# Strassen's algorithm in the first channel product of two more chunks, with turns between VectorE and GpSimd

## The chip, the core and the metric

The kernel runs on one core of one Trainium2 chip. Five engines run beside each other, each with its own queue of instructions that it works off in order: TensorE (PE; its weight loads are shown as PEld), VectorE (DVE), ScalarE (ACT), GpSimd (POOL) and SyncE (SP). They wait for each other by semaphores. Only TensorE multiplies matrices, and it writes to PSUM; VectorE and ScalarE read PSUM, GpSimd works in SBUF alone. The metric is the device time of one execution in microseconds.

## What is computed

The reference is a linear attention with random features (8 batches, 8 heads, 576 positions, head size 64, 128 features), followed by a mixer over tokens and over channels:

```python
def phi(x):
    proj = np.einsum('bhsd,md->bhsm', x, omega)
    sq = np.sum(x * x, axis=-1, keepdims=True) / 2.0
    h = proj - sq
    h = h - np.max(h, axis=-1, keepdims=True)
    return np.exp(h) / np.sqrt(m)
q_p, k_p = (phi(q_s), phi(k_s))
kv = np.einsum('bhsm,bhsd->bhmd', k_p, v)
z = np.sum(k_p, axis=2)
num = np.einsum('bhsm,bhmd->bhsd', q_p, kv)
den = np.einsum('bhsm,bhm->bhs', q_p, z)[..., None] + 1e-06
x = num / den                                # heads side by side: 576 x 512 for each batch
h = np.maximum(x.T @ w_tok1, 0.0) @ w_tok2   # tokens, 576 -> 256 -> 576
u = x + h.T
out = u + np.maximum(u @ w_ch1, 0.0) @ w_ch2 # channels, 512 -> 1536 -> 512
```

## The kernel before

Matrices are held in fp16, sums in fp32. For each batch b there are three stages. **Attention** (`attention`): for each of four pairs of heads, TensorE projects k and q (`kp`, `qp`, lines 679 and 691) and the last 64 positions (`kt`, `qt`, 571 and 641); ScalarE takes the exponentials; VectorE takes the largest entry (`km`), GpSimd scales v by its reciprocal (`vs_`, by the helper in line 315); TensorE forms `kv` (735, 742) and the numerators (768, 770), and VectorE or ScalarE divides. **Token mixing** (`token_mix`): lines 796 and 803, a relu, line 816, and `uadd` on VectorE; a SyncE transpose (`ut_dma`) turns `u` into `uT`; `token_tail` (870) does the last 64 positions of two batches. **Channel mixing** (`channel_mix`): 512 positions of a batch make a chunk, and the 64 left over from each of eight batches make a ninth, so there are nine, c = 0 to 8.

The first channel product of a plain chunk is 12 blocks of four matmuls of 512 columns (line 1144), each with one relu from PSUM (helper lines 310 and 312). From c = `FAST_IN` on it goes by `channel_in_fast`: the product is cut in two by two by two, four sums of `uT` blocks are made (`go`, engine chosen, helper line 315), then seven products of four matmuls of 256 columns in each of three parts (line 1073 records those matmuls and line 1097 the joins). ScalarE copies three products out of PSUM (`keep`), VectorE adds them to others (`join`), and relus work from PSUM or within SBUF. It needs eight sums of blocks of `w_ch1` (`weight_sums`), made once; they take the place of one of three q slots and one of three k slots. From c = 1 on the second product goes by a Strassen form too, with eight sums `S` of relu outputs for each chunk (`channel_out_fast`, line 961; reads in line 941); four sums of `w_ch2` blocks (line 468) are made once. Chunk 0 uses lines 1150, 1152 and 1178.

From batch 2 on, q and k come in by two DMAs: GpSimd issues a cast from fp32 to a DRAM scratch (for k one for the main part and two small ones for the tail), and SyncE issues a transpose back to SBUF (`qT`, `kT`, line 400). GpSimd also issues the loads of v and its tails (lines 357 and 371).

The order of all work is written out by hand. `Planner.add` makes numbered jobs, each with an engine, dependencies and buffers; `ORDER` lists their numbers, `SLOT` the buffer that each takes, `MOVED` the jobs whose engine is not the usual one. `Planner.run` emits them in the order of `ORDER`, so each engine's queue is its part of that list. Negative numbers are dummy matmuls that fill the start.

Of the kernel before, what the change touches and what calls it, by code (L numbers as in the profile page):

```python
# [92 lines left out]
]  # L93
# [44 lines left out]
class Planner:  # L138
# [8 lines left out]
    def add(self, eng, cost, key, fn, deps=(), take=(), give=(), rows=False, wire=0.0):  # L147
        job = Job(eng, cost, key, fn, [d for d in deps if d is not None], list(take), list(give), rows, wire)
        self.jobs.append(job)
        return job  # L150

    warm = None

    def run(self):
        slots = iter(SLOT)
# [30 lines left out]
def kernel(  # L186
# [12 lines left out]
    nc = tc.nc  # L199
# [135 lines left out]
    ld = {}  # L335
# [915 lines left out]
```

## Time and profile before

| what | value |
|---|---|
| three runs | 274.83, 275.26, 275.27 us; median 275.26 |
| the profiled execution | 273.79 us, of which the span of the trace is 272.0 |
| granted TensorE clock | 0.998 |
| VectorE / ScalarE / GpSimd busy | 227.2 / 164.2 / 134.6 us |
| DMA | 39.70 MB, mean 146 GB/s |

A line of the profile names a line of the kernel, an engine, an operation and the tiles it writes and reads; "x28" is a count. Matmuls are pipelined, so the mean time of one is longer than the spacing from one to the next; the chain of waits, which gives the time of a run of matmuls, shows the spacing. Helper lines (306, 310, 312, 315, 534) stand for many uses, which are told apart by tile and shape.

### The profile page before, as it was taken

How to read it: one execution, taken by the hardware profiler on the slowest of the kernel's cores; microseconds unless marked ns; L12 is line 12 of the kernel's file. 1: busy time of each engine (PE TensorE's matmuls, PEld its weight loads, DVE VectorE, ACT ScalarE, POOL GpSimd, SP SyncE). 2: the span in 40 equal slices, each digit the busy share in tenths (PEclk: the TensorE clock that was granted, in tenths of full speed). 3: DMA queues.
4: the chain of work that ended last, by engine and by line, in shares of the span. 5: the costliest groups of instructions: out<-in, count | busy, mean ns of one | idle time of the engine just before them, and what ended most of it. 6: DMA issues, size and time to landing. Idle time of an engine off the chain costs nothing.

```text
span 272.0 us, 6648 instructions
## 1 busy us (share of the span) xinstructions
PE 262.9 (97%) x2647; PEld 180.0 (66%) x2647; DVE 227.2 (84%) x479; ACT 164.2 (60%) x361; POOL 134.6 (49%) x146
## 2 busy tenths in 40 slices
PE   7799999999999999999999999999999999999992
PEld 4367455444568655766578546986789688888881
DVE  3897879876998799987889799899997795799992
ACT  2999941188695338736746865699947541573500
POOL 8895492064803490079459996964145044600001
PEclk9999999999999999999999999999999999999999
DMA  8999999999999999989989986980260063030134
GB/s 199 190 208 210 191 210 185 216 202 132 180 204 156 223 187 175 164 160 158 171 178 173 194 233 64 182 167 2 49 128 2 23 193 58 0 157 0 63 133 119
DMA packets 81296, 39.70 MB, mean 146 GB/s; under 512 B 63984, under 2 KB 77040, under 8 KB 81072
## 3 DMA queue, kind: packets, MB, share of 16 engines
q0 software_dynamic: 31744, 17.74, 44.2%
q1 hardware_dynamic: 46928, 15.37, 29.5%
q10 hardware_dynamic: 2592, 6.16, 6.4%
q8 instruction: 20, 0.33, 0.5%
q14 instruction: 12, 0.10, 0.1%
HBM read 35.95 MB, written 16.52 MB: 193 GB/s over the span
## 4 chain that ended last, share of the span: by engine, by line
PE 86%; DMA 8%; POOL 3%; DVE 1%; issue 0%; POOLq 0%; SPq 0%
PE bank L961 24%; PE bank L1144 19%; PE bank L1073 13%; PE bank L803 5%; PE bank L816 5%; DMA uT<-u 4%; DMA w1m<-in_moe_w_tok_dram 4%; PE bank L1178 4%; PE bank L679 3%; PE bank L768 3%; PE bank L735 3%; PE bank L691 2%; POOL r L339 1%; PE bank L870 1%; PE bank L842 1%; PE bank L854 1%
## 5 line engine op out<-in xcount | busy, mean ns | idle before, releaser
L1144 PE MATMUL bank<-uT,wc 128*128 128x512 f16 x232 | 56.0, 379 | 0.0
L315 POOL TENSOR_TENSOR vs<-v,vs 128x512 f16<-128x512 f16 x31 | 33.1, 1072 | 42.8 <-DVE vs L716 33.5
L310 ACT ACTIVATE r<-bank 128x512 f16<-128x512 f32 (+1 forms) x61 | 34.5, 598 | 26.5 <-PE bank L1144 16.0
L961 PEld LDWEIGHTS <-r 128*128 128x128 f16 x384 | 36.7, 98 | 7.2 <-issue 1.6
L534 ACT ACTIVATE kp<-bank 128x512 f16<-128x512 f32 x64 | 35.5, 623 | 9.6 <-PE bank L679 8.9
L712 DVE TENSOR_REDUCE km<-kp 128x8 f16<-128x1024 f16 x32 | 38.5, 1204 | 2.0 <-ACT kp L534 2.0
L534 ACT ACTIVATE qp<-bank 128x512 f16<-128x512 f32 x64 | 36.5, 620 | 4.3 <-PE bank L691 4.3
L1144 PEld LDWEIGHTS <-wc 128*128 128x128 f16 x232 | 20.5, 98 | 20.1 <-issue 1.1
L961 PEld LDWEIGHTS <-S 128*128 128x128 f16 x288 | 27.7, 98 | 4.7 <-issue 0.4
L786 DVE TENSOR_TENSOR x<-bank,rc 128x320 f16<-128x320 f32 x53 | 25.2, 483 | 1.1
L941 DVE TENSOR_TENSOR o<-u,bank 128x512 f32<-128x512 f16 x28 | 19.1, 680 | 5.8 <-PE bank L961 5.3
L961 PE MATMUL bank<-T,r 128*128 128x256 f16 x192 | 23.8, 273 | 0.0
L961 PE MATMUL bank<-T,S 128*128 128x256 f16 x192 | 23.4, 272 | 0.0
L961 PE MATMUL bank<-wc,r 128*128 128x256 f16 x192 | 23.1, 273 | 0.0
L312 DVE TENSOR_SCALAR r<-bank 128x512 f16<-128x512 f32 (+1 forms) x29 | 18.9, 661 | 3.1 <-PE bank L1144 2.4
L819 DVE TENSOR_TENSOR u<-x,bank 128x512 f16<-128x512 f16 x28 | 17.9, 681 | 1.9 <-PE bank L816 1.9
L315 POOL TENSOR_TENSOR vbd<-vt,vbd 128x512 f16<-128x512 f16 x6 | 6.4, 1060 | 23.5 <-DVE vbd L616 18.5
L768 PEld LDWEIGHTS <-qp 128*128 128x128 f16 x256 | 14.0, 98 | 5.9 <-issue 0.3
L1073 PE MATMUL bank<-uT,wc 128*128 128x256 f16 x120 | 16.6, 273 | 0.6 <-DMA uT<-u 0.6
L941 DVE TENSOR_TENSOR o<-o,bank 128x512 f32<-128x512 f32 x21 | 14.3, 680 | 3.1 <-PE bank L961 2.9
L775 DVE RECIPROCAL rc<-bank 128x5 f32<-128x5 f32 x64 | 11.2, 184 | 6.7 <-PE bank L770 3.7
L768 PE MATMUL bank<-kvsb,qp 128*128 128x65 f16 x256 | 16.0, 193 | 0.2 <-ACT qp L534 0.2
(151 smaller groups left out, 551.3 us busy)
## 6 DMA issues: line engine op xcount, KB each, us to landing
out_dram<-o ACTq DMA_DIRECT2D x9, 512.0 KB, 3.7
q<-in_q_dram POOLq DMA_DIRECT2D x6, 576.0 KB, 7.6
wc<-in_moe_w_ch_dram POOLq DMA_DIRECT2D x4, 768.0 KB, 11.1
k<-in_k_dram POOLq DMA_DIRECT2D x6, 512.0 KB, 7.1
v<-in_v_dram POOLq DMA_DIRECT2D x6, 512.0 KB, 8.6
out_dram<-o SPq DMA_DIRECT2D x5, 512.0 KB, 3.1
r<-in_q_dram POOLq DMA_DIRECT2D x4, 288.0 KB, 7.1
v<-in_v_dram POOLq DMA_DIRECT2D x4, 256.0 KB, 8.9
```

What stands on the lines that cost most here:

```text
L310: nc.scalar.activation(out=out, in_=in_, func=AF.Relu)
L312: nc.vector.tensor_relu(out=out, in_=in_)
L315: (nc.gpsimd if eng == "POOL" else nc.vector).tensor_tensor(**kw)
L534: nc.scalar.activation(out=out, in_=in_, func=AF.Exp, bias=0.0, scale=1.0)
L712: nc.vector.reduce_max(out=t_km[place("km", (b, hp))], in_=src_, axis=AX.X)
L768: nc.tensor.matmul(ps[:, k, j * 65 : (j + 1) * 65], st, s[:, i, 0 : D + 1], start=True, stop=True)
L786: nc.vector.tensor_tensor(out=to, in0=ps, in1=rc.unsqueeze(2).broadcast_to((P, NJ + 1, D)), op=ALU.mult)
L819: nc.vector.tensor_tensor(out=t_u[place("u", b)][:, j, :], in0=t_x[place("x", b)][:, j, :], in1=bank(n), op=ALU.add)
L941: nc.vector.tensor_tensor(out=o, in0=a, in1=ps, op=ALU.add)
L961: nc.tensor.matmul(ps[:, j * DH : (j + 1) * DH], a[:, cb, j * P : (j + 1) * P], w[:, cb, :], start=(bank_of(b, j0) not in held and j == j0 ...
L1073: nc.tensor.matmul(ps[:, n, :], w(a)[:, (2 * m + n) * P : (2 * m + n + 1) * P], x_[:, a], start=(what in ("P1", "P2", "P5") and n == 0 and ...
L1144: nc.tensor.matmul(ps, wc1[:, db, cb * P : (cb + 1) * P], moving(db), start=(db == 0), stop=(db == ND - 1))
```

## The change

1. `FAST_IN` goes from 5 to 3: chunks 3 and 4 take `channel_in_fast` as well. With c = 5 to 8 that makes six of nine.
2. Jobs that read and write SBUF alone carry `port=True`: the sums `S`, the input sums, the weight sums, the relus within SBUF, and from batch 2 on the mask product, `vbd` and `vs_`. When such a job on one of VectorE and GpSimd is emitted, its first instruction is made to wait for the last such instruction that the other engine was given before it in the order, unless that was waited for already. This gives 53 waits: 26 of VectorE for GpSimd, 27 of GpSimd for VectorE.
3. `ORDER`, `SLOT` and `MOVED` are new from the end of batch 1's attention on. Before that only the banks of three groups of dummy matmuls change.

What differs by count of jobs (engine by engine):

| job | VectorE | ScalarE | GpSimd | TensorE |
|---|---|---|---|---|
| output sums `S` | 54 to 36 | | 10 to 28 | |
| input sums of `uT` | 3 to 11 | | 13 to 13 | |
| weight sums | 0 to 3 | | 8 to 5 | |
| products of the fast first stage | | | | 84 to 126 |
| `keep` | | 36 to 54 | | |
| `join` | 36 to 54 | | | |
| relus of the fast first stage | 12 to 22 | 24 to 32 | | |
| plain blocks of line 1144 | | | | 58 to 34 |
| their relus | 21 to 14 | 39 to 22 | | |
| `kv` copies, divisions, token relus | 69 to 63 | 41 to 47 | | |

The weight sums now begin right after the sums of `w_ch2` blocks, during batch 1's token mixing. Three places of the new queues:

- GpSimd, after the load of v of batch 2: a weight sum, which by its turn waits for VectorE's first weight sum; two tail casts of k of batch 3; a weight sum; the main cast of k of batch 3. TensorE's first use of that `kT` is `kt` of batch 3, among chunk 1's blocks.
- GpSimd, in chunk 1's output sums: one sum, the load of v of batch 3, two sums that need the relu of chunk 1's last block, the tail casts of k of batch 4. Its first use, `kp` of batch 4, stands behind chunk 1's product number seven.
- GpSimd, in chunk 2's output sums: tail casts of k of batch 6, the load of v of batch 5, a sum which waits its turn for chunk 3's last input sum, then a tail of v, the main cast of k of batch 7, a tail of v, tail casts of batch 7, a tail of v, the main cast of k of batch 6. First use: `kp` of batch 6, behind batch 4's token mixing.

```diff
-    def add(self, eng, cost, key, fn, deps=(), take=(), give=(), rows=False, wire=0.0):
+    def add(self, eng, cost, key, fn, deps=(), take=(), give=(), rows=False, wire=0.0, port=False):
         job = Job(eng, cost, key, fn, [d for d in deps if d is not None], list(take), list(give), rows, wire)
+        job.port = port
         self.jobs.append(job)
         return job
...
+    def turns(self, tc, nc):
+
+        engines = {"DVE": mybir.EngineType.DVE, "POOL": mybir.EngineType.Pool}
+        last = {}
+        after = mybir.DependencyInfo(mybir.DependencyClass.Sync, mybir.DependencyReason.DATA)
+        def go(job):
+            traced = nc.cur_bb.bb.instructions
+            n = len(traced)
+            job.fn()
+            if not job.port or job.eng not in engines:
+                return
+            new = [i for i in nc.cur_bb.bb.instructions[n:] if i.engine == engines[job.eng]]
+            other = last.get("POOL" if job.eng == "DVE" else "DVE")
+            if other is not None:
+                tc.add_manual_dep(new[0], other, after, reason="shared port")
+                last["POOL" if job.eng == "DVE" else "DVE"] = None
+            last[job.eng] = new[-1].name
+        self.go = go
...
-            j.fn()
+            self.go(j)
...
-    FAST_IN = 5
+    FAST_IN = 3
...
-                job = add(e_sum, 0.5, key + KEYS["S"] + 0.1 * g + 0.01 * k, go, deps=[*need, *([done[2 if k == 3 else 0]] if k else [])], take=[("S", c)])
+                job = add(e_sum, 0.5, key + KEYS["S"] + 0.1 * g + 0.01 * k, go, deps=[*need, *([done[2 if k == 3 else 0]] if k else [])], take=[("S", c)], port=True)
...
+    plan.turns(tc, nc)
     plan.run()
```

More of the change, by code (lines that the diff above doesn't have):

```diff
@@ L34 @@
     282, 283, 358, 179, 264, 198, 181, 34, 233, 267, 199, 234, 235, 231, 232, 284, 188, 265, 266, 193, 268, 269,
[58 rows of a table removed]
[61 rows of a table added]
 ]
 SLOT = (
-    "0100234050600701103402521706330511460210051223125233033711610240602131270511342163750420056150672712"
-    "4605012137512011365072310230040171020353162243332500316157113242670140235273510446726122030716211530"
-    "7621001035170301612430750012215233641100337415107203005261712324105603750146637054100201605373160221"
-    "3417034617220102300111410160112206212373120413000601312612072013361501345061372705416110302172426125"
-    "0604507130102321004112560270223610715300247200023170141501702032545031703240514062231700400322171045"
-    "1630001075212431053730213210145021011523301212643571030160001741260005120136543035461200711622730510"
-    "0462010341720112126245172201331264025010007101214723236350421705243520532047661402771131116005027134"
-    "6012520463170425116120203004715211601405130720326031400562210513204760123120501236071104220156031131"
-    "71007022247131421062510023034007621125"
+    "0100234050600701103402521706330411560210041223124233033711610250603121207411353126040437052140673012"
+    "5204713106413711024063317200050161037340122250333407012146110052260152204363517456732122006012034206"
+    "0112004512014603230510141121151420235233010325061020417312116252100326541710123150434662015207174621"
+    "0123005436001230112322251340111623050116220154211006022524117603021526747406153206714010530032175621"
+    "4322230107232615370315120060750131021160412201131761151321322204625602725301126051000062151007236143"
+    "2100150174322123135026700124611002507036040310151126074102215110400123304712462013170267302053200101"
+    "3271130205760131002220531060410072232110154361071206302340157164107113202500172761036245560343703011"
+    "3506211470332472121670020403751100621050127310062000167234107612031622707605471011070014570134152001"
+    "6710232732011762530700460315211304201035170402"
 )
@@ L107 @@
     122: "ACT", 128: "ACT", 139: "ACT", 147: "DVE", 149: "DVE", 153: "DVE", 157: "ACT", 159: "DVE", 167: "DVE",
-    171: "DVE", 173: "DVE", 175: "ACT", 179: "DVE", 185: "DVE", 191: "ACT", 197: "ACT", 206: "ACT", 207: "ACT",
-    208: "DVE", 229: "ACT", 246: "ACT", 289: "DVE", 314: "DVE", 322: "DVE", 350: "ACT", 396: "DVE", 413: "DVE",
-    439: "DVE", 466: "DVE", 468: "DVE", 472: "DVE", 474: "DVE", 527: "DVE", 544: "DVE", 606: "DVE", 610: "DVE",
-    616: "DVE", 620: "DVE", 628: "POOL", 629: "POOL", 630: "POOL", 632: "POOL", 647: "ACT", 648: "ACT",
@@ L112 @@
-    677: "DVE", 694: "DVE", 697: "ACT", 728: "DVE", 731: "ACT", 739: "DVE", 750: "DVE", 758: "DVE", 764: "DVE",
-    770: "DVE", 772: "DVE", 776: "POOL", 780: "POOL", 795: "ACT", 828: "ACT", 848: "ACT", 876: "DVE", 879: "ACT",
-    899: "POOL", 900: "POOL", 901: "POOL", 902: "POOL", 903: "POOL", 904: "POOL", 905: "POOL", 906: "POOL",
-    907: "POOL", 908: "POOL", 909: "POOL", 910: "POOL", 925: "ACT", 926: "ACT", 942: "ACT", 958: "ACT",
-    962: "POOL", 981: "ACT", 1011: "DVE", 1017: "ACT", 1028: "DVE", 1051: "ACT", 1062: "DVE", 1083: "POOL",
@@ L117 @@
-    1084: "POOL", 1085: "POOL", 1086: "POOL", 1100: "DVE", 1101: "ACT", 1117: "ACT", 1118: "ACT", 1133: "ACT",
-    1134: "ACT", 1135: "POOL", 1139: "POOL", 1142: "POOL", 1157: "ACT", 1158: "ACT", 1190: "ACT", 1238: "DVE",
-    1244: "ACT", 1261: "POOL", 1262: "POOL", 1263: "POOL", 1264: "POOL", 1278: "DVE", 1294: "DVE", 1311: "ACT",
-    1312: "ACT", 1335: "ACT", 1336: "ACT", 1342: "POOL", 1359: "ACT", 1360: "ACT", 1376: "ACT", 1391: "ACT",
+    171: "DVE", 173: "DVE", 175: "ACT", 179: "DVE", 185: "DVE", 196: "ACT", 197: "ACT", 201: "ACT", 207: "ACT",
@@ new lines @@
+    208: "DVE", 229: "ACT", 246: "ACT", 308: "DVE", 320: "DVE", 326: "DVE", 327: "POOL", 328: "POOL", 329: "POOL",
+    330: "POOL", 331: "POOL", 334: "POOL", 350: "ACT", 379: "DVE", 396: "DVE", 441: "DVE", 458: "DVE", 462: "DVE",
+    468: "DVE", 470: "DVE", 474: "DVE", 478: "POOL", 479: "POOL", 480: "POOL", 481: "POOL", 527: "DVE",
+    533: "ACT", 544: "DVE", 564: "ACT", 567: "ACT", 581: "ACT", 589: "DVE", 602: "POOL", 603: "POOL", 604: "POOL",
+    605: "POOL", 607: "POOL", 627: "ACT", 643: "ACT", 660: "ACT", 662: "POOL", 664: "POOL", 668: "POOL",
@@ new lines @@
+    683: "ACT", 684: "ACT", 736: "ACT", 747: "DVE", 767: "ACT", 785: "POOL", 786: "POOL", 787: "POOL", 818: "DVE",
+    820: "ACT", 837: "POOL", 838: "POOL", 840: "POOL", 843: "POOL", 844: "POOL", 859: "ACT", 909: "ACT",
+    923: "DVE", 929: "ACT", 964: "POOL", 965: "POOL", 966: "POOL", 981: "ACT", 982: "ACT", 998: "ACT",
+    1014: "ACT", 1016: "POOL", 1018: "POOL", 1022: "POOL", 1037: "ACT", 1107: "ACT", 1118: "DVE", 1139: "POOL",
+    1140: "POOL", 1141: "POOL", 1157: "ACT", 1174: "ACT", 1194: "POOL", 1196: "POOL", 1198: "POOL", 1213: "ACT",
@@ L121 @@
+    1214: "ACT", 1260: "DVE", 1263: "ACT", 1277: "DVE", 1297: "ACT", 1336: "ACT", 1350: "DVE", 1351: "ACT",
+    1352: "ACT", 1368: "ACT", 1372: "POOL", 1376: "POOL", 1391: "ACT", 1392: "ACT", 1397: "POOL", 1398: "POOL",
+    1399: "POOL", 1400: "POOL", 1414: "DVE", 1415: "ACT", 1432: "ACT", 1447: "ACT", 1452: "POOL", 1456: "POOL",
 }
@@ L621, in kt_mask @@
                 )
-            j_ktm = add("DVE", 0.15, kkt + 0.01, kt_mask, deps=[j_ktm, j_msk], take=take_vbd, give=[("kmt", b)])
+            j_ktm = add("DVE", 0.15, kkt + 0.01, kt_mask, deps=[j_ktm, j_msk], take=take_vbd, give=[("kmt", b)], port=b >= 2)
             def vbd():
@@ L631, in attention @@
             e_vbd = engine("POOL")
-            j_vbd = add(e_vbd, 1.05 if dma_in else 1.95, kkt + 0.02, vbd, deps=[j_ktm, *ld["vt", b]], give=[("vt", b)])
+            j_vbd = add(e_vbd, 1.05 if dma_in else 1.95, kkt + 0.02, vbd, deps=[j_ktm, *ld["vt", b]], give=[("vt", b)], port=b >= 2)
         j_tail = [j_vbd0, *j_kte] if b == 0 else [j_vbd]
@@ L703, in attention @@
             if b in HALVES:
-                j_h = [add("DVE", 0.35, at_["km"], km_half, deps=je, take=[("vs", (b, hp))])]
+                j_h = [add("DVE", 0.35, at_["km"], km_half, deps=je, take=[("vs", (b, hp))], port=True)]
             else:
@@ L727, in vs_ @@
                 )
-            j_v = add(e_vs, 1.07, at_["vs"] - (6.0 if b == 0 else 0.0), vs_, deps=[j_m, ld["v", b, hh[0]], ld["v", b, hh[1]]], give=[("v", b)])
+            j_v = add(e_vs, 1.07, at_["vs"] - (6.0 if b == 0 else 0.0), vs_, deps=[j_m, ld["v", b, hh[0]], ld["v", b, hh[1]]], give=[("v", b)], port=b >= 2)
             def kv(hp=hp, n_kv=n_kv):
@@ L951, in base_in @@
                 tt(e_base, out=o, in0=t_u[place("u", c)][:, 2 * i : 2 * i + 2, DH * e : DH * e + DH], in1=o, op=ALU.add)
-            return add(e_base, 1.1, key + KEYS["c2"] + step * k, base_in, deps=deps, give=[("u", c)])
+            return add(e_base, 1.1, key + KEYS["c2"] + step * k, base_in, deps=deps, give=[("u", c)], port=True)
         outs, j_z = {}, {}
@@ L1028, in weight_sums @@
                 n = 2 * i + a
-                done.append(add(e_sum, 0.46, key, go, deps=[*need, *j_wc1], take=[("qT" if n < 3 else "kT", "sums")] if n < 6 else []))
+                done.append(add(e_sum, 0.46, key, go, deps=[*need, *j_wc1], take=[("qT" if n < 3 else "kT", "sums")] if n < 6 else [], port=True))
             j_sums.append(done)
@@ L1043, in go @@
                 tt(e_sum, out=sums()[:, i], in0=a(), in1=b(), op=ALU.subtract)
-            j_s.append(add(e_sum, 0.35, key, go, deps=[*jt, *([j_s[i // 2]] if i % 2 else [])], take=[("uT", ("sums", c))]))
+            j_s.append(add(e_sum, 0.35, key, go, deps=[*jt, *([j_s[i // 2]] if i % 2 else [])], take=[("uT", ("sums", c))], port=True))
         half_c = DC // 2
@@ L1119, in relu1 @@
                 relu_to(e_relu, t, t)
-            c1 = add(e_relu, 0.35, kk, relu1, deps=[c11, c12], take=[("r3", c)])
+            c1 = add(e_relu, 0.35, kk, relu1, deps=[c11, c12], take=[("r3", c)], port=True)
             e_relu = engine("DVE")
@@ L1123, in relu22 @@
                 relu_to(e_relu, r3(1, 1, m), r3(1, 1, m))
-            c2 = add(e_relu, 0.2, kk, relu22, deps=[c22], take=[("r3", c)])
+            c2 = add(e_relu, 0.2, kk, relu22, deps=[c22], take=[("r3", c)], port=True)
             for n in range(2):
```

125 rows, old and new, of the table ORDER are left out of this document.

## The prediction

> **What bounds the kernel now.** I read the page first, then each engine's busy time over the long middle, TensorE's waits there, and the chain of waits for the price of one step.
>
> ```profile
> PE 262.9 (97%) x2647; PEld 180.0 (66%) x2647; DVE 227.2 (84%) x479; ACT 164.2 (60%) x361; POOL 134.6 (49%) x146
> PE 86%; DMA 8%; POOL 3%; DVE 1%; issue 0%; POOLq 0%; SPq 0%
> 55.00:267.00 212.00, 211.35 (x2076) 150.75 (x2071) 183.54 (x383) 129.87 (x281) 100.87 (x98) 1.00 0.72 132
> 74.30:211.70 137.40, 137.06 (x1400) 94.16 (x1396) 120.94 (x258) 92.42 (x213) 77.11 (x74) 1.00 0.85 148
> PE bank L1073 <- DMA uT<-u: 0.6, 2, 0.3
> PEld L1073 <- DMA uT<-u: 0.5, 1, 0.5
> ```
>
> From 55 to 267 us TensorE is busy 211.35 of 212.00 us at a granted clock of 1.00, and the only wait of its own worth naming is about 1 us for two transposed `uT` tiles. So matmul time taken out there comes off the end in full, as long as nothing new arrives late; by the same rows there is no slack to hide a late operand in. VectorE is next: 120.94 of 137.40 us between 74.3 and 211.7, that is 88%.
>
> The unit prices, from the chain of waits (start, time, instruction, count):
>
> ```profile
> 47.34 0.32 PE bank L796 x2
> 47.67 1.83 PE bank L803 x8
> 49.50 1.73 PE bank L1178 x8
> 51.23 1.73 PE bank L816 x8
> 55.12 0.45 PE bank L679 x16
> 59.37 0.55 PE bank L870 x4
> 59.92 0.32 PE bank L691 x2
> 66.80 0.24 PE bank L735 x8
> 67.05 0.06 PE bank L742
> 68.27 0.12 PE bank L768 x4
> 68.39 0.03 PE bank L770
> 74.10 0.22 PE bank L641 x2
> 81.82 0.22 PE bank L571 x4
> 117.51 4.32 PE bank L1144 x20
> 234.62 10.04 PE bank L1073 x92
> 253.84 13.11 PE bank L961 x120
> ```
>
> **TensorE.** A plain chunk has 48 matmuls of 512 columns at 4.32/20 = 0.216 us; by Strassen it has 7 x 12 = 84 of 256 columns at 10.04/92 = 0.1091. For chunks 3 and 4: 96 x 0.216 = 20.74 us go, 168 x 0.1091 = 18.33 come, **-2.4 us**, all on the path. The changed warm-up matmuls only swap banks: nothing.
>
> **The other engines.** Rows by shape (busy, mean ns | idle before):
>
> ```profile
> L1097 DVE TENSOR_TENSOR r<-r,bank 128x512 f16<-128x512 f32 x12 | 8.1, 680 | 1.0 <-PE bank L1073 0.9
> L315 DVE TENSOR_TENSOR S<-S,r 128x768 f16<-128x768 f16 x16 | 8.8, 553 | 0.1
> L315 DVE TENSOR_TENSOR uT<-uTt 128x512 f16<-128x512 f16 x2 | 0.8, 418 | 0.0
> L312 DVE TENSOR_SCALAR r<-bank 128x512 f16<-128x512 f32 x27 | 18.1, 679 | 2.7 <-PE bank L1144 2.4 <-PE bank L803 0.2
> L312 DVE TENSOR_SCALAR r<-r 128x1024 f16<-128x1024 f16 x5 | 2.0, 420 | 0.0
> L315 POOL TENSOR_TENSOR S<-r 128x768 f16<-128x768 f16 x3 | 4.9, 1637 | 13.5 <-PE bank L961 11.1 <-ACT r L310 2.4
> L310 ACT ACTIVATE r<-bank 128x512 f16<-128x512 f32 x59 | 33.8, 605 | 26.5 <-PE bank L1144 16.0 <-PE bank L803 10.1 <-issue 0.2
> ```
>
> VectorE gains 18 joins (12.2 us), 8 input sums (3.3), 10 relus within SBUF (at most 0.42 each, 4.2) and 3 weight sums (1.7), 21.4 us; it loses 18 output sums (9.9), 7 chunk relus (4.8) and some 6 small PSUM reads, which I price at 0.42 each, 2.5: 17.2 us. So **+4 us** on VectorE. GpSimd gets 18 output sums and gives up 3 weight sums: 15 x 1.637 = **+25 us**, of 137 us that it is idle now. ScalarE gets 18 copies and 8 relus for 17, some 9 at 0.605 and a few more: +5 to +9, of 108 idle. By totals all of it fits; 88% on VectorE becomes some 91% in the middle. For the lost overlaps I take +0.6 us.
>
> **The turns.** Counted in the new order, 53 waits: 26 of a VectorE sum for a GpSimd sum, 27 the other way. Behind a waiting VectorE sum stand the joins and PSUM reads, for which TensorE waits; behind a waiting GpSimd sum stand the casting loads of q, k and v, for which SyncE's transposes and then TensorE wait. What a collision costs without turns is shown once (VectorE, then GpSimd):
>
> ```profile
> 158.34 1.08 DVE L616 TENSOR_TENSOR vbd<-kmt,mask 128x8 f16<-128x8 f16 x1
> 157.74 1.64 POOL L315 TENSOR_TENSOR sum<-wc,qT 128x768 f16<-128x768 f16 x1
> ```
>
> The tiny mask product ends at 159.42, 0.04 us after GpSimd's sum, so a sum that comes second is held until the other has ended, and a semaphore makes it wait for the same end. So a turn adds only where the written order differs from the order of readiness: between -0.9 us (a collision of this kind avoided) and +1.64 (a whole GpSimd sum) each; I take nothing beyond the 0.6 above. The Trainium skill, SBUF — State Buffer, section "Who interferes with whom", has the same lock, and its Perfetto Trace Analysis, section "Optimizing Scalar/DVE Operations", warns that moving work between these two may not help; by that warning the 18 moved sums gain VectorE nothing, and it would stand at +14 us and not at +4. The row agrees on the lock; the warning is weighed as a rival below.
>
> **The loads in the new order** decide. Now TensorE waits for no k tile; in the new order three of them stand hard against their first use. Landing times, issue costs, and VectorE's last sum of W2 blocks:
>
> ```profile
> k<-in_k_dram POOLq DMA_DIRECT2D x6, 512.0 KB, 7.1
> k<-in_k_dram POOLq DMA_DIRECT2D x12, 32.0 KB, 6.8
> kT<-k SPq DMA_TRANSPOSE x6, 6.5
> DMA to landing us min/median/max: 5.0/6.5/9.0
> L371 POOL DMA_DIRECT2D vt<-in_v_dram x16 | 10.7, 674 | 0.3 <-POOL vbd L315 0.3
> L390 POOL DMA_DIRECT2D k<-in_k_dram x12 | 10.2, 856 | 0.0
> L384 POOL DMA_DIRECT2D k<-in_k_dram x6 | 3.5, 576 | 0.0
> 48.34 0.95 DVE L468 TENSOR_TENSOR T<-wc,T 128x1536 f16<-128x1536 f16 x1
> ```
>
> *Batch 3.* The first weight sum (0.55) follows that sum: 49.84. GpSimd waits for it (a turn), does a weight sum, two tail casts, a weight sum (2 x 1.64 + 2 x 0.86): 54.84. Cast of k: 61.9; transpose: 68.4. TensorE, from 47.34: one L796 0.32, two L803 groups 1.83, four of L816 1.73, seven thirds of L1178 6.05, four kp 1.8, three qp 0.96, kt and qt 0.44, token tail 0.55, eight blocks of chunk 1 6.92, two kv 0.6: 21.2, so 68.5. On time by 0.1; with the transpose's ends 1.6 early to 2.4 late.
>
> *Batch 4.* Its tail cast stands on GpSimd behind two output sums of chunk 1 that need that chunk's last relu. From the end of that block: relu 0.61, two sums 3.27, first tail issued 0.86, landing of the second 6.8, transpose 6.5: 18.0; a load of v and another sum before them can add some 0.7. TensorE has until its first use six numerators 0.9, kp 1.8, four qp 1.28, six output products 7.87, L796 0.32, L803 1.83, qt 0.22, L816 1.73, four kv 1.2: 17.15. **Late by 0.9 to 1.6**; with the transpose's ends -0.6 to +4.1.
>
> *Batch 6.* Its cast stands behind an output sum of chunk 2 that waits its turn for chunk 3's last input sum; between are four issues of 0.67 to 0.86, another cast and a third v tail. From that input sum: 0.42 + 1.64 + 3 x 0.67 + 2 x 0.86 + 0.58 + 7.1 + 6.5 = 20.0, and 0.9 for the load ahead of the sum if GpSimd is behind; TensorE has 13 products 5.67, six output products 7.87 and attention and token parts 7.2: 20.8. On time by the median, but the cast now follows another of 512 KB at once: between 1.3 early and 3 late.
>
> Early pays nothing and late is paid in full, so places near zero cost on average half their scatter: I take 0.3, 1.5 and 1.0, **+2.8 us**. The two late `uT` of now stay.
>
> **Sum.** -2.4 + 0.6 + 2.8 = **+1.0 us**. The profiled execution took 273.79 us (272.0 span and 1.8 around it), 0.5% under the median of 275.26 of the three runs; its sum would give 274.8, and on the median **276.3 us**.
>
> **Rivals.** *Faster.* The three tiles land at the short ends of their rows and stay hidden; the same cast-and-transpose chains end in time all through the present trace, where TensorE waits for no kT. Then -2.4 is left, or -1.0 with one place 1.4 late: 272.9 to 274.5. It decides below 1.8 us of lateness in all. For it speaks that VectorE's and GpSimd's totals fit; against, that batch 4 is late by its medians. *VectorE bound.* The 26 turns hold VectorE 0.5 us each on average, half of the collision's 0.9 or somewhat more: 13 us, and the 4 added, against 28.5 us that it is idle from 55 to 267, most of which is waiting for TensorE. Some 2 us of it then reach TensorE on top of the loads: 278 to 279. The page's warning is this case. *A wash.* The loads give back just the 2.4: 274.7 to 275.8.
>
> **How the numbers follow.** About 0.2% (0.55 us) can be told from no change. Forecast (late kT tiles, +0.6 to +3) 0.38; VectorE bound 0.12; both slower: 0.50. Faster 0.40, a wash 0.10. Likeliest case's own range 275.9 to 278.3; holding 8 in 10 takes most of the faster case and the start of the VectorE case: 273.0 to 278.6.
>
> **What would show it.** Right: TensorE's idle time before L679 or L571, released by `kT<-k`, some 2 to 4 us in all; the Strassen products of the first stage at 504 matmuls (336 now) of 0.109 us; VectorE's busy time up by about 4, GpSimd's by 25. Wrong: no such wait and a span of 269.6 (loads early), or waits of L961 and L1073 for VectorE or GpSimd sums of several us (turns).

## The result, and the profile after

The kernel after took 277.29 us (median of 17 runs, 275.08 to 283.88), the kernel before beside it 274.83. The ratio is 1.0086 with a 95% interval of 1.0059 to 1.0112: slower by some 2.4 us. The forecast was 276.3, and 1.0 us more than before. Two more comparisons of the same kernel gave 276.54 us (ratio 1.0059, 1.0033 to 1.0085) and 277.89 (1.0114, 1.0069 to 1.0159); the ratios leave out executions more than 1.5% above the fastest of their kernel, which the medians include.

The profiled execution took 278.06 us with a span of 276.3. The change moves the line numbers used here by 24: 679 is now 703, 961 is 985, 1073 is 1097, 315 is 339. From its page, busy time by engine and the chain of waits:

```profile
PE 263.5 (95%) x2719; PEld 187.5 (68%) x2719; DVE 228.5 (83%) x487; ACT 173.5 (63%) x384; POOL 158.0 (57%) x161
PE 67%; DMA 14%; POOL 7%; DVE 7%; SPq 2%; issue 2%; POOLq 0%; DVEq 0%
```

There are 72 matmuls more, 168 for 96, as the change says. The chain of waits, 86% TensorE before, is 67% TensorE now, and what came in is DMA, GpSimd and VectorE. TensorE's own waits (us in all, times, longest) name the operands:

```profile
PE bank L531 <- DMA r<-in_q_dram: 1.9, 2, 1.6
PE bank L703 <- DMA kT<-k: 1.7, 2, 1.2
PE bank L1168 <- DMA uT<-u: 1.4, 1, 1.4
PE bank L1097 <- DVE r L1121: 0.4, 1, 0.4
PE bank L595 <- DVE u L843: 0.4, 1, 0.4
```

The first line is a load of q some 10 us after the start, ahead of the new order. It is 0.2 us in the kernel before, and the two later profiles of the kernel after don't have it. The two waits for `kT` are batch 4's (1.2) and batch 2's; the `uT` is batch 1's, which the first product of channel chunk 1 reads. None of these last four lines is in the kernel before, whose two short waits for a `uT` (0.6 in all) are gone here. The same by stretch of time, before first, then the second profile of the kernel after, whose span is 275.1 us (us; busy PE, PEld, DVE, ACT, POOL; granted clock; DMA):

```profile
47.00:77.00 30.00, 30.00 (x256) 14.98 (x254) 23.80 (x49) 19.10 (x39) 12.38 (x15) 1.00 1.20 189
77.00:107.00 30.00, 30.00 (x285) 19.21 (x282) 26.50 (x56) 16.87 (x35) 11.92 (x15) 1.00 1.07 188
107.00:160.00 53.00, 53.00 (x543) 34.23 (x542) 46.17 (x98) 34.07 (x86) 34.86 (x32) 1.00 1.01 177
160.00:190.00 30.00, 30.00 (x316) 21.69 (x315) 27.20 (x58) 22.94 (x52) 21.69 (x20) 1.00 0.66 113
```

```profile
47.00:77.00 30.00, 27.96 (x239) 13.83 (x237) 21.04 (x43) 17.57 (x37) 18.63 (x19) 1.00 1.19 200
77.00:107.00 30.00, 28.92 (x313) 18.51 (x310) 25.60 (x56) 22.46 (x57) 23.03 (x23) 1.00 1.18 172
107.00:160.00 53.00, 52.98 (x581) 40.97 (x579) 48.70 (x107) 38.86 (x90) 34.01 (x32) 1.00 1.04 179
160.00:190.00 30.00, 29.07 (x310) 20.75 (x309) 27.65 (x60) 22.53 (x49) 18.37 (x16) 1.00 0.52 97
```

The idle time lies where the loads are dense (2.04 and 1.08 us) and at two places near 164 and 168 us (0.93 together); 107 to 160 is as full as before.

The balance is best taken from the first matmul of batch 1's token mixing (L796, now L820), about where the new order begins, to the start of the last matmul. That stretch took 219.4 us before, 221.9 in the first profile and 222.0 in the second: 2.5 and 2.6 us more. The Strassen products should save 2.4 of matmul spacing, so some 5.0 us were lost. The wait lists name 3.3 and 3.4 us more than before in this stretch (3.9 and 4.0 for 0.6). The remaining 1.5 or so has no row in them. 0.5 of it follows the `qp` matmuls (L691, now L715), which take 6.0 us from their starts to those of the next matmuls before and 6.5 in both profiles. And the first channel products of chunks 1 to 8 went from 79.1 us, taken in the same way, to 77.0: 2.15 less and not 2.4. The rest I leave open.

The first profile also came to that first matmul 1.95 us late (49.23 us for 47.28), with the wait for q and a granted clock of 0.83 in its first 20 us, where the order of work is unchanged but for dummy matmuls. The second has 1.00 there and was 0.6 late, the third 0.1, so I put most of that to the one execution and not to the change.

### The profile page after: what moved, and what is told of

The parts are those of the page before. It is cut to its first block, busy times and chain, and to the rows that moved or that the text cites. A ratio compares the mean times of both kernels' runs of the same rounds, so it can differ in the third digit from the quotient of the medians.

```text
span 276.3 us, 6861 instructions
## 1 busy us (share of the span) xinstructions
PE 263.5 (95%) x2719; PEld 187.5 (68%) x2719; DVE 228.5 (83%) x487; ACT 173.5 (63%) x384; POOL 158.0 (57%) x161
## 4 chain that ended last, share of the span: by engine, by line
PE 67%; DMA 14%; POOL 7%; DVE 7%; SPq 2%; issue 2%; POOLq 0%; DVEq 0%
PE bank L985 22%; PE bank L1097 17%; PE bank L1168 8%; DMA uT<-u 3%; DMA v<-in_v_dram 3%; POOL vs L339 3%; PE bank L715 3%; PE bank L827 3%; DMA k<-in_k_dram 3%; DMA kT<-k 2%; PE bank L840 2%; DMA r<-in_q_dram 2%; PE bank L792 2%; SPq L424 2%; PE bank L759 2%
## 5 line engine op out<-in xcount | busy, mean ns | idle before, releaser
L334 ACT ACTIVATE r<-bank 128x512 f16<-128x512 f32 (+1 forms) x51 | 30.2, 609 | 23.0 <-PE bank L827 9.7
L339 POOL TENSOR_TENSOR S<-r,S 128x768 f16<-128x768 f16 x15 | 24.5, 1642 | 31.5 <-PE bank L985 8.7
L985 PEld LDWEIGHTS <-r 128*128 128x128 f16 x384 | 36.7, 98 | 5.2 <-issue 0.4
L1168 PE MATMUL bank<-uT,wc 128*128 128x512 f16 x136 | 32.1, 379 | 1.4 <-DMA uT<-u 1.4
L985 PEld LDWEIGHTS <-S 128*128 128x128 f16 x288 | 27.5, 98 | 4.9 <-DVE S L339 0.7
L1097 PE MATMUL bank<-uT,wc 128*128 128x256 f16 x192 | 26.2, 273 | 0.0
L810 DVE TENSOR_TENSOR x<-bank,rc 128x320 f16<-128x320 f32 x51 | 24.2, 483 | 1.0
L985 PE MATMUL bank<-T,r 128*128 128x256 f16 x192 | 23.6, 273 | 0.0
L985 PE MATMUL bank<-T,S 128*128 128x256 f16 x192 | 23.5, 273 | 0.0
L1168 PEld LDWEIGHTS <-wc 128*128 128x128 f16 x136 | 12.5, 98 | 15.8 <-DMA uT<-u 1.8
L985 PE MATMUL bank<-wc,r 128*128 128x256 f16 x192 | 23.1, 273 | 0.0
L1097 PEld LDWEIGHTS <-wc 128*128 128x128 f16 x216 | 20.4, 98 | 3.1 <-issue 0.3
L1097 PE MATMUL bank<-uT,qT 128*128 128x256 f16 x108 | 19.0, 273 | 0.0
L330 ACT COPY qp<-bank 128x512 f32<-128x512 f32 x18 | 10.4, 603 | 13.0 <-PE bank L1097 13.0
L1097 PE MATMUL bank<-uT,kT 128*128 128x256 f16 x108 | 18.5, 272 | 0.0
L339 POOL TENSOR_TENSOR r<-r 128x768 f16<-128x768 f16 x6 | 9.9, 1646 | 12.6 <-DVE S L339 6.7
```

Of the source, the lines that this page charges most:

```text
L330: (nc.scalar.copy if eng == "ACT" else nc.vector.tensor_copy)(out=out, in_=in_)
L334: nc.scalar.activation(out=out, in_=in_, func=AF.Relu)
L339: (nc.gpsimd if eng == "POOL" else nc.vector).tensor_tensor(**kw)
L810: nc.vector.tensor_tensor(out=to, in0=ps, in1=rc.unsqueeze(2).broadcast_to((P, NJ + 1, D)), op=ALU.mult)
L985: nc.tensor.matmul(ps[:, j * DH : (j + 1) * DH], a[:, cb, j * P : (j + 1) * P], w[:, cb, :], start=(bank_of(b, j0) not in held and j == j0 ...
L1097: nc.tensor.matmul(ps[:, n, :], w(a)[:, (2 * m + n) * P : (2 * m + n + 1) * P], x_[:, a], start=(what in ("P1", "P2", "P5") and n == 0 and ...
```

## Experiments

The first comparison held the kernel after itself, unaltered:

> The changed kernel, unaltered, for a second profile and as the mark for the three beside it. Late loads: 276.5 to 278, with TensorE waiting again some 1.5 us for the first transposed uT and over 1 us for batch 4's kT. If the 1.9 us by which the first profile was behind before the new order even begins (47.3 to 49.2 us at batch 1's token mixing) was chance, this profile has less of it; if the swapped banks of the dummy matmuls cause it, it is there again.

Measured: 276.54 us; its profile is the second one above, with a wait of 2.0 us for `uT`, 1.1 for batch 4's `kT` and 0.5 for the join.

The kernel numbers its jobs, and most edits move numbers in the list that sets the order; the fragments show only what moved. Times are medians; each ratio is to runs of the kernel before on the same chip.

**The turns taken out of the new order.**

```diff
-    plan.turns(tc, nc)
+    plan.go = lambda job: job.fn()
```

> The 53 waits between VectorE and GpSimd left out, all else as changed. Late loads: GpSimd no longer stands 7.3 us before its first weight sum, so batch 3's casts go out that much earlier, and batch 4's hardly; 0.5 to 2 us faster than the changed kernel, 275 to 276.5. VectorE bound by the turns: most of the loss goes, 272.5 to 274. Turns that avoid collisions: slower than the changed kernel, by 0.9 us for each few collisions, 278 or more.

Measured: 299.0 us, ratio 1.0882 (1.0828 to 1.0936). VectorE's busy time went from 228.7 to 246.6 us. Its sums in the second profile of the kernel after, and without turns (busy, mean ns | idle before):

```profile
L339 DVE TENSOR_TENSOR S<-S,r 128x768 f16<-128x768 f16 x13 | 7.0, 553 | 0.4 <-POOL S L339 0.3
L339 DVE TENSOR_TENSOR r<-r 128x768 f16<-128x768 f16 x10 | 5.4, 550 | 1.6 <-POOL S L339 1.5
```

```profile
L339 DVE TENSOR_TENSOR S<-S,r 128x768 f16<-128x768 f16 x13 | 12.3, 962 | 0.2
L339 DVE TENSOR_TENSOR r<-r 128x768 f16<-128x768 f16 x10 | 11.1, 1113 | 0.0
PE bank L703 <- DMA kT<-k: 8.5, 1, 8.5
PE bank L985 <- DVE S L339: 3.2, 2, 2.5
kT<-k SPq DMA_TRANSPOSE x1, 14.9
```

The same instructions take up to twice as long, VectorE stands 19.4 us above the kernel before, and TensorE waits for it (L985). That is what the Trainium skill says in SBUF — State Buffer, section "Who interferes with whom": a VectorE operation with two inputs in SBUF and a GpSimd one that reads SBUF exclude each other. There is a second loss in it, and not one of sums: 8.5 us for batch 2's `kT`, whose transpose took 14.9 us (last line, from issue to landing). The first of the 53 turns makes GpSimd's first weight sum wait 7.3 us; without it, batch 3's casts behind it start at 44.1 us and not at 52, and run beside that transpose.

**Only the first turn kept**, to part the two.

```diff
-            if other is not None:
+            if other is not None and "first" not in last:
+                last["first"] = True
```

> The changed kernel with the first of its 53 turns kept (GpSimd's first weight sum behind VectorE's first) and the other 52 left out. Without any turn it took 299.0 us, and TensorE waited 8.7 us for batch 2's kT, whose transpose ran beside batch 3's casts, let go 5 us earlier. Theory that this one wait and the collisions of sums share the 22 us: the wait for batch 2's kT is gone (under 1 us), VectorE stays at 244 to 248 us busy with its S<-S,r sums near 960 ns, and the time is 287 to 293. Rival, that the late casts are nearly all of it: 277 to 281. Rival, that the collisions are nearly all: 295 to 300.

Measured: 289.76 us (284.23 to 293.45), too scattered for a ratio, so I read the trace: span 286.8, VectorE busy 245.7, and the wait for batch 2's `kT` gone. Against spans of 295.7 without turns and 275.1 with all, the first turn is worth some 9 us, by holding loads back, and the other 52 some 12, by keeping sums apart. By the fastest executions of the three (296.61, 284.23 and 275.20 us) it is 12 and 9. So there are two shares of like size, as the theory had it; how they divide is known only roughly.

**The turns in the old order**: the kernel after with the order, buffers and `FAST_IN` of the one before.

```diff
-    FAST_IN = 3
+    FAST_IN = 5
```

> The kernel before with the turns of the changed kernel alone: its own order, its own product by twelve matmuls on the sixth chunk, GpSimd's and VectorE's sums made to take turns. Theory that the turns are worth what they cost only in an order laid out for them (they save some 22 us in the new order: 299.0 without, 276.5 with): the old order keeps the sums apart by itself (VectorE's 128x768 sums took 550 ns there, as undisturbed ones do), so the turns can only add waits: 274.5 to 278, with waits of VectorE on GpSimd sums of 1 to 4 us in the profile. Rival, that the turns are a gain in any order: below 273.8. Rival, that they bind VectorE's in-order queue hard: above 280.

Measured: 289.88 us, ratio 1.0539 (1.0492 to 1.0587), 15 us slower; my 274.5 to 278 was far off, and the rival that the turns bind VectorE's queue held. Waits of VectorE and TensorE (lines stand 20 behind those of before):

```profile
DVE S L335 <- POOL vbd L335: 6.6, 1, 6.6
DVE S L335 <- POOL uT L335: 4.4, 1, 4.4
PE bank L981 <- DVE o L961: 5.7, 2, 3.9
PE bank L981 <- DVE S L335: 3.4, 1, 3.4
```

One VectorE sum of the second channel stage waits 6.6 us for a GpSimd `vbd` that stands earlier in the list but comes late in time; TensorE then stands still for 3.9 us. The turns are neither cheap nor dear: each enforces the written order, 15 us lost in an order written without them, 22 saved in one written for them.

**k(4)'s tail cast earlier**, against the wait for batch 4's `kT`.

```diff
-    ... 202, 687, 378, ... 572, 575, 686, 441, ...
+    ... 202, 687, 686, 378, ... 572, 575, 441, ...
```

> Batch 4's two tail casts of k are issued right behind its main cast, ahead of chunk 1's last output sums; nothing else moves. Late loads: the wait for batch 4's kT (1.3 us in the first profile) goes and the time falls by 0.8 to 1.5 us against the changed kernel. VectorE bound: no change, within 0.3 us.

Measured: 277.7 us, ratio 1.0069 (1.004 to 1.0098). The wait for `kT` is gone from the trace, whose span fell to 274.3, but the ratio is no better than that of the kernel after in the same comparison (1.0059). The mechanism is right; that its removal gains a microsecond isn't shown.

**k(3)'s casts earlier.**

```diff
-    ... 358, 179, ... 603, 500, 361, ... 368, 501, 325, ...
+    ... 358, 500, 501, 179, ... 603, 361, ... 368, 325, ...
```

> Batch 3's casts of k are issued right behind batch 2's load of v, ahead of the weight sums and their wait for VectorE. Late loads: they land before the first uT transpose (which took 8.8 us beside them, 5.65 before) begins, its wait of 1.6 us goes, and the time falls by 1 to 1.6 us against the changed kernel; less if they delay batch 2's transposes instead. VectorE bound: no change, within 0.3 us.

Measured: 282.56 us, ratio 1.0253 (1.0197 to 1.0308), and the gain that I expected failed; the exception that it named came instead. Batch 1's `uT` was no longer late, but the casts now ran beside batch 2's transposes:

```profile
PE bank L703 <- DMA kT<-k: 6.8, 1, 6.8
```

**Part of batch 3's casts later** (q's and the tails of v; k's stay).

```diff
-    ... 375, 505, 323, 316, 363, 499, 317, ... 318, 504, 426, ... 365, 411, ... 394, 307, ...
+    ... 375, 323, 316, 363, 317, ... 318, 426, ... 365, 499, 411, ... 394, 505, 504, 307, ...
```

> The changed kernel with batch 3's q cast moved on GpSimd's queue behind batch 2's vbd sum, and batch 3's two vt casts behind batch 2's vs sums; k's casts stay, since batch 3's kT is used 1.1 us after it lands. Theory that the casts running beside batch 1's uT transpose (8.8 to 9.1 us to land, 5.65 in the kernel before) make it late: it lands at 60.5 to 62 us, TensorE's wait of 2.2 us before batch 1's uT products falls to 0 to 1, and the time is 0.8 to 2 us below the changed kernel's 276.5. Rival, that the k casts or the q transpose on SyncE's queue are what it shares with: still 1.8 to 2.4 us of wait and the same time. Rival, that q's late cast moves the wait to batch 3's qT (used at 77.3 us): a new wait there of about 1 us.

Measured: 278.79 us, ratio 1.0134 (1.0093 to 1.0176). `uT` still took 9.4 us, so the first rival held: q's and v's casts don't make it late. The same with k(4)'s tail cast early as well:

> As the run with batch 3's q and vt casts later, and batch 4's tail cast of k moved right behind its main cast, which by itself took away the wait of 1.25 us for batch 4's kT. Theory that these two waits are what the change lost in TensorE's stream: both gone, 1.5 to 3 us below the changed kernel's 276.5, so 273.5 to 275.0, level with the kernel before or a little under. Rival, that the time is made elsewhere (stream slack is taken back by the next late tile): 276 to 277.5.

Measured: 277.63 us, ratio 1.0102 (1.0066 to 1.0139); `uT` still late by 1.9 us, a new wait of 0.6 for batch 2's `kT`, none for batch 4's. The rival held.

**All of batch 3's casts behind the landing of `uT`**, batch 3's `kt` products later.

```diff
-    ... 603, 500, 361, ... 368, 501, 325, 375, 505, 323, ... 363, 499, 317, ... 318, 504, 426, 364, 365, 411, ... 503, 507, ...
+    ... 603, 361, ... 368, 325, 375, 323, ... 363, 317, ... 318, 426, 411, 500, 501, 499, 364, 365, ... 394, 505, 504, ... 303, 507, 509, 508, 510, 511, 512, ...
```

> The changed kernel with all of batch 3's casts let go later: k's three and q's one behind batch 2's first vs sum on GpSimd's queue (about 60.8 us, when batch 1's uT should have landed), the vt casts behind its last vs sum; batch 3's four kt matmuls with their exponentials and reciprocals are moved behind the last product of channel chunk 1, so that kT(3) may land 4 us later. Moving the q and vt casts alone left uT's landing at 62.65 us. Theory that it is k's casts (14 and more descriptors' work from 51 to 64 us) that lie beside uT's transpose: it lands at 59 to 61 us, 5.5 to 6.5 us after its issue, TensorE's wait of 2.1 to 2.4 us falls under 0.7, kT(3) or qT(3) costs at most 1 us at 74 to 78 us, and the time is 274.5 to 276 where the changed kernel takes 276.5. Rival, that uT's transpose is slowed by the transpose of q that runs ahead of it in the same queue: still lands at 62 to 63 us, 276 to 278.

Measured: 291.98 us, ratio 1.0555 (1.0509 to 1.0601). The transpose of `uT` (us from issue to landing) before, in the third profile of the kernel after, and here with what followed:

```profile
uT<-u SPq DMA_TRANSPOSE x1, 5.6
```

```profile
k<-in_k_dram POOLq DMA_DIRECT2D x1, 512.0 KB, 8.4
uT<-u SPq DMA_TRANSPOSE x1, 11.2
```

```profile
uT<-u SPq DMA_TRANSPOSE x1, 4.5
kT<-k SPq DMA_TRANSPOSE x1, 12.9
qT<-q SPq DMA_TRANSPOSE x1, 15.5
PE bank L595 <- DMA kT<-k: 7.7, 1, 7.7
PE bank L715 <- DMA qT<-q: 6.0, 1, 6.0
```

With no cast beside it `uT` took 4.5 us, and TensorE didn't wait for it: the theory of its lateness held. The price was not foreseen: batch 3's `kT` and `qT`, moved back, met batch 4's casts and took 12.9 and 15.5 us (the second queued behind the first). My "at most 1 us" there was 13.7. The Trainium skill, DMA: Bandwidth & Descriptors, section "Queues, rings and completion order", has each DMA engine take turns between its queues packet by packet; that fits a transpose that slows down beside casts, though no run here looks inside an engine.

**The same, with k(4)'s tail cast early and one turn moved** behind the two joins that it held up at 163 us.

```diff
-    ... 807, 788, 1053, 951, 831, 948, 814, 832, 815, ...
+    ... 807, 951, 831, 948, 814, 832, 788, 1053, 815, ...
```

> As the run with all of batch 3's casts behind batch 1's uT, with two more edits: batch 4's tail cast of k right behind its main cast (the wait for kT(4) of 1.25 us went with that edit before), and VectorE's fourth sum of chunk 4's uT, whose turn made VectorE wait 1.17 us for a GpSimd vs sum with two joins queued behind it, moved behind these joins, GpSimd's vbd sum behind it as before. Theory that the waits found in the trace are the whole difference to the kernel before: TensorE's idle time falls from 21 to 17 us, the span to 271.5 to 272.5, the time to 273.0 to 274.5, level with the kernel before (274.5) or under it. Rival, that freed time is taken back by the next late operand in the same stream: 275.5 to 277.

Measured: 296.02 us, ratio 1.0556 (1.0512 to 1.0599). With two casts more beside it, `kT` of batch 3 took 18.1 us and TensorE waited 12.6 for it, in the trace of an execution of 295.99 us; the fastest took 289.81. The moved turn did what it should: no wait of L1097 for a join is left.

**The kernel after once more**, on the chip of these two.

> The changed kernel unaltered, for the comparison on the same chip and a third profile of it: 275.5 to 277.5, with waits for batch 1's uT of 1.5 to 2.3 us, for kT(4) of 1.2 to 1.4 us, and of 0.5 to 0.8 us at 163 and at 168 us in each profile if these are of the order and not of chance; if they are chance, another set of waits.

Measured: 277.89 us. The waits are at the same places: `uT` 4.1, batch 4's `kT` 1.5, the join 0.7, `u` 0.4 us. So the places belong to the order. The size of the first does not: 1.4, 2.0 and 4.1 us in three traces.

**Casts spread out**, every move together.

```diff
-    ... 411, 376, ... 692, 407, 202, 687, ... 862, ... 506, ... 686, ...
+    ... 411, 501, 499, 364, 365, 376, ... 407, 202, 687, ... 686, ... 506, 692, ... 862, ...
```

> The changed kernel with the casts spread over the stretch from 50 to 85 us instead of all behind uT: k(3)'s tail cast stays where it is (52 us), its main cast and q(3)'s go behind batch 2's first vs sum (62 us), vt(3)'s behind the last vs sum; batch 3's kt matmuls behind the last product of channel chunk 1; batch 4's tail cast of k takes the place of batch 5's, and the other way round; batch 4's v cast goes behind batch 3's; VectorE's fourth sum of chunk 4's uT and GpSimd's vbd sum behind the two joins. Moving all casts behind uT let uT land 4.5 us after its issue, but then kT(3) took 12.9 us and qT(3) 15.5 us beside batch 4's casts. Theory that every transposition's time is set by the casts beside it, and that the new order can be helped by spreading them: uT lands at 59 to 61 us, kT(3) by 75, qT(3) by 78, kT(4) is no longer late, TensorE's idle time is 16.5 to 18.5 us and the time 273.0 to 275.0. Rival, that the stretch has no room: one of kT(3), qT(3) or kT(4) is late by 2 us or more, and the time is 276 to 280.

Measured: 282.91 us, ratio 1.0303 (1.0266 to 1.034). Batch 3's `kt` products stand as in the two runs with all casts behind `uT`, and the moved turn as in the second of them. Batch 1's `uT` and batch 4's `kT` were on time, and `qT` of batch 3 late instead; batch 2's `kT` was 0.9 late. The rival, that the stretch has no room, held, with a time even above its 276 to 280:

```profile
PE bank L715 <- DMA qT<-q: 4.1, 1, 4.1
qT<-q SPq DMA_TRANSPOSE x1, 10.3
```

No version here beats the kernel before.

## Why the prediction was right

**TensorE, -2.4.** Right: 72 matmuls more, with 504 Strassen products of the first stage in place of 336, still 0.109 us apart; in place the saving was 2.15 us.

**The other engines.** GpSimd +25: measured +23.4 (158.0 for 134.6). ScalarE +5 to +9: +9.3. VectorE +4: +1.3. The joins came as sized (36 to 54 of them, 24.2 to 36.2 us). Part of the miss is that the turns freed the small mask products, of which one was my example of a collision:

```profile
L616 DVE TENSOR_TENSOR vbd<-kmt,mask 128x8 f16<-128x8 f16 x6 | 2.3, 386 | 0.1
```

```profile
L640 DVE TENSOR_TENSOR vbd<-kmt,mask 128x8 f16<-128x8 f16 x6 | 1.1, 185 | 0.0
```

**Lost overlaps, +0.6.** The waits for a join and for `u` are 0.4 and 0.4 us in the first trace, 0.7 and 0.4 in the third. The join's comes from a turn: VectorE's fourth sum of chunk 4's `uT` waits for a GpSimd `vs` sum (time, then idle before it), with two joins behind it, and moving it took the wait away.

```profile
162.93 0.42 DVE L339 TENSOR_TENSOR uT<-uT,uT 128x512 f16<-128x512 f16 x1 [1.17 <-POOL vs L339]
```

**The turns, nothing beyond that.** Right in the sum, wrong as a general price. I held that a semaphore only makes a sum wait for the end that the lock would make it wait for. For the old order I worked out 0 to 3.5 us by it, and 15 were measured; I had no price for a turn whose partner is late for reasons of its own. And I took collisions as rare, since the kernel before shows few; in the new order they would have cost some 9 to 12 us, and VectorE more than the 14 us that the prediction set beside the warning on moving work between these two engines.

**The loads, +2.8.** Right in kind, and by the working for one place of three. Batch 4's `kT`, foreseen 0.9 to 1.6 late, was 1.1 to 1.5 late, off a transpose of 6.80 us at 88.85, just behind its cast. Batch 6's, for which I took 1.0, was never late. Batch 3's was on time, but by luck:

```profile
63.59 3.82 SPq L424 DMA_TRANSPOSE kT<-k  x1
kT<-k SPq DMA_TRANSPOSE x1, 6.7
71.42 0.29 PE L595 MATMUL bank<-omT,kT 64*128 64x128 f16 x4
```

In the second profile it landed at 70.3 us, 1.1 ahead of its first use, and TensorE had stood still 2.0 us before that for `uT`. Without that wait it would have been some 0.9 late, as an estimate from these rows. In the first profile it was 1.0 ahead, after 1.9 us of such waits.

My sign of being right, 2 to 4 us of waiting for `kT`, was not met: it was 1.7, 1.1 and 1.5 us in the three profiles. What brought the sum near the forecast is a tile that I had excluded with "the two late `uT` of now stay". Those two all but went, and batch 1's `uT` came late by 1.4 to 4.1 us. The step that failed was to follow only the chains that end in the moved casts, and not the transposes that they now run beside.

**The rivals.** *Faster* and *A wash* fell with the late tiles. *VectorE bound* is not what happened, VectorE being idle for 48 of 276 us, but its mechanism ruled where the turns met an order not made for them.

**The size.** Forecast +1.0, measured +2.4 by the medians. In the first two profiles the waits alone rose by 3.3 and 3.4 us, and 3.4 had been taken for lost overlaps and loads together; that they agree is luck, as `uT` made up for what `kT` fell short. What the forecast lacks is the 1.5 us or so that no wait row names. A clock effect, told below, adds to the third profile, but not to the first two.

## What to carry to other kernels

When loads move in an order written by hand, don't price only whether the moved load still lands in time: list the transposes that will be in flight beside it, and price each at the slow end. A semaphore that keeps two engines off a shared port is worth what the written order makes of it: lay out the order with it, and look at what stands behind the waiting instruction. And a stretch whose DMA engines are full may have no free place for a cast: each of the six orders here that moved batch 3's casts left `uT` late or made another transpose late. Only moving batch 4's tail cast by itself took a wait away without a new one, and the ratio didn't show it.

## What the hardware showed that I had not expected

**The time of a transpose depends on what runs beside it**, far beyond the 5.0 to 9.0 us that the kernel before shows for six transposes of `kT`: 4.5 us for a `uT` with no cast beside it, 8.8 to 11.2 beside one batch's casts, 12.9 to 18.1 for a `kT` beside another's.

**A wait can cost again after it ends.** TensorE around the late `uT` in the third profile (wait 4.1 us), in the run with q's and v's casts later (2.3), and in the second profile (2.0); the column before the last two is the granted clock:

```profile
60.50:64.80 4.30, 0.23 (x2) 0.00 (x0) 1.39 (x5) 1.05 (x2) 2.06 (x2) 1.00 1.08 200
64.80:68.60 3.80, 3.76 (x10) 1.37 (x11) 0.72 (x1) 1.08 (x2) 0.00 (x0) 0.55 1.24 191
```

```profile
60.00:62.70 2.70, 0.42 (x6) 0.09 (x3) 1.57 (x5) 1.23 (x3) 1.15 (x2) 1.00 0.74 182
62.70:66.80 4.10, 4.10 (x12) 1.58 (x13) 1.71 (x4) 1.08 (x2) 1.70 (x3) 0.59 0.88 141
```

```profile
60.50:63.10 2.60, 0.56 (x7) 0.23 (x5) 1.71 (x5) 1.38 (x3) 0.89 (x1) 1.00 1.36 287
63.10:67.00 3.90, 3.90 (x19) 1.76 (x20) 1.68 (x4) 1.92 (x4) 1.37 (x3) 1.00 1.01 140
```

After the two longer waits the clock stood near half for about 4 us, ten to twelve matmuls where nineteen ran otherwise: some 1.7 us more lost. After 2.0 us it stayed full; in the run with q's and v's casts later and k(4)'s tail cast early, a wait of 1.9 us brought it down (0.57 over 4.0 us). And in the run with the turns in the old order, the wait of 3.4 us for a sum `S` left it full:

```profile
208.90:210.60 1.70, 1.68 (x18) 1.44 (x19) 0.47 (x1) 0.00 (x0) 1.15 (x1) 1.00 0.00 0
```

So between 1.9 and 3.4 us it falls or not. The Trainium skill, TensorE: Matmul & The Clock Gate, section "What's actually happening", has the clock halve after an idle window of about 3.4 us; the half and the time to recover agree, but here 1.9 us of idleness were once enough. It also has that window run freely, which would fit that waits of nearly one length end both ways. This may be why the kernel after scatters more than the one before, since its wait for `uT` lies at this edge; with one trace for each of three runs that is argued, not shown.

Left open: how much of the 2.4 us each late tile accounts for over many runs, as no edit that took a wait away was clearly faster than the kernel after; and where the rest of the 1.5 us that no wait row names comes from.
